# Gated linear-attention block with a gated feed-forward: output products in pairs on two row tiles, denominators in pairs, side work given to engines by a table, and a new order

## The chip, the cores and the metric

The kernel runs on one NeuronCore of a Trainium2 chip. Five engines work side by side, each through its own instructions in order: TensorE (PE in the profile, its weight loads PEld), VectorE (DVE), ScalarE (ACT), GpSimd (POOL) and SyncE (SP, which here only issues DMA). They wait for one another by semaphores. The metric is the time of one execution on the device in microseconds (us); less is better.

## The reference

Four batches (B = 4), eight heads (H = 8), 768 tokens, head size 40. Per batch and head a recurrent memory C (40 x 40) and a normaliser n are carried over the tokens, with gates that are stabilised by a running maximum m:

```
m_new  = max(f + m, i);  f_stab = exp(f + m - m_new);  i_stab = exp(i - m_new)
C = f_stab * C + i_stab * outer(v, k);   n = f_stab * n + i_stab * k
y = sigmoid(o) * (C q) / max(|n . q|, 1)
```

Then a feed-forward over x = y with the heads laid side by side (320 columns): `gate = sigmoid(causal depthwise convolution of x over 5 tokens)`, `out = (gate * (x @ w_val)) @ w_out`.

## The kernel before

The 768 tokens are cut into six blocks of 128 tokens (j0 to j5), and a block into two parts of 64 tokens (p0, p1). For each block and batch (24 pairs, u = 4j + b) the recurrence is computed part by part (g = 2u + p) in its matrix form. The scaled q and k are split into an fp16 high and low part and stacked (`prep_max`, `prep_scale`, `prep_hi`, `prep_lo`; `hi` runs on ACT or POOL, `lo` on DVE), and turned so that head channels lie on partitions, either by TensorE (`turn_pe`, copied out of PSUM by `turn_out`) or by a DMA transpose from SyncE's queue (`prep_tr`, L397); the function `TURN` says which. Then for each part: `args` (one matmul with the gate logarithms, L417), `expo` (Exp on ACT, L420), `scores` (8 matmuls, L430), `probs` (DVE, scores times decays, L435), `keyw` (POOL, keys times decays, L442), `heads` (L459 and L461: per head the output product and the update of the carried state, in two column halves of the TensorE array), and `state_out` (ACT copies the new state from PSUM back into SBUF, L468), on which the same batch's next part depends.

After both parts of a batch: `norm` (three small DVE instructions on 8 columns, L473 to L475: max(|n.q|, scale), reciprocal), `norm_o` (POOL, output gate times reciprocal, L479), `gate_o` (DVE, L482), `x_tr` (three transposes on TensorE, L489), `x_copy` (two ACT copies out of PSUM, L496 and L497).

The feed-forward of a block runs later, among the attention of later blocks: `conv` (the first of five taps on ACT, L526, the others on DVE, L528), `sigmoid`, `val` (L557 to L569), `z_mul` (DVE, L574), and per batch `outp`: two full 128-row products (L579) and the 64 channels that are left, which `outp` multiplies as a 128-row product as well for blocks j0 to j4, because `wo3` holds zeros in the other 64 rows (L581). Only in the last block, j5, which is fed in two halves of two batches, is the third product cut to 64 rows. `outp_st` (ACT, L584) copies the result to one of three buffers and `out_dma` (SyncE, L587) stores it.

The weights come as 64-bit floats and are converted on DVE, POOL and ACT (L602 to L609). Gate logarithms are built by DVE (`gates`), sent through DRAM by small DMAs on ACT's queue (`spread_g`, `spread_a`) and gathered again on SyncE's.

The whole order is written out by hand: each operation has a kind, and `PLAN` gives every instance of a kind a rank. The operations are issued in order of rank, and so each engine's queue is in that order. `BANKS` does the same for the eight PSUM banks. For most kinds the engine is fixed in the code.

## Time and profile before

| | us |
|---|---|
| median of three runs (239.35 to 240.8) | 240.64 |
| the profiled execution, its own time | 239.06 |
| span of the profiled execution, first to last instruction | 237.3 |
| busy in the span: TensorE / VectorE / ScalarE / GpSimd | 191.2 / 188.5 / 170.5 / 114.8 |
| mean granted TensorE clock, of full speed | 0.892 |

A profile is one execution. The time outside its span is 239.06 - 237.3 = 1.76 us. Matmuls are pipelined, so that TensorE counts as busy also where the next matmul could have started earlier; start-to-start distances say more than durations there. DVE instructions overlap a little as well.

### The profile page before, as it was taken

What the parts mean: (1) busy time and instruction counts of PE and PEld (TensorE: products, weight loads), DVE (VectorE), ACT (ScalarE), POOL (GpSimd) and SP (SyncE); (2) the same over time, 40 slices, a digit from 0 to 9 for tenths busy, and PEclk for the clock granted to TensorE, in tenths of its full rate; (3) what the DMA queues carried; (4) which work ended last, traced back from release to release, by engine and by line L of the source; (5) the groups of instructions that cost most, each with busy time, mean ns of one, the idle gap of its engine ahead of it and who ended that gap; (6) DMA issues with size and microseconds to landing.
All of it is one profiled execution on the core that took longest, in us unless ns stands there. A gap on an engine that the chain in (4) does not pass through costs nothing.

```text
span 237.3 us, 6304 instructions
## 1 busy us (share of the span) xinstructions
PE 191.2 (81%) x2392; PEld 138.9 (59%) x2392; DVE 188.5 (79%) x433; ACT 170.5 (72%) x353; POOL 114.8 (48%) x171
## 2 busy tenths in 40 slices
PE   0025075599951599999999999999999999999994
PEld 0024053598831576767776687677677866876541
DVE  7999989879997799789996899588966496549920
ACT  5738539978789997698998888797575827339131
POOL 8998550868877656444677184417624020220000
PEclk9999555579995555999999999999999999999999
DMA  6999955999999995999999999999794110011002
GB/s 130 155 191 163 126 79 104 181 195 123 170 181 177 179 181 75 197 175 174 197 156 187 219 179 167 211 182 157 169 172 91 42 70 3 7 51 57 3 32 79
DMA packets 146662, 31.95 MB, mean 135 GB/s; under 512 B 142472, under 2 KB 145928, under 8 KB 146632
## 3 DMA queue, kind: packets, MB, share of 16 engines
q1 hardware_dynamic: 145000, 31.25, 83.7%
q10 hardware_dynamic: 1632, 0.30, 0.9%
q8 instruction: 19, 0.31, 0.6%
q14 instruction: 11, 0.09, 0.1%
HBM read 17.87 MB, written 4.23 MB: 93 GB/s over the span
## 4 chain that ended last, share of the span: by engine, by line
PE 62%; ACT 14%; DVE 9%; issue 4%; SPq 4%; POOL 2%; DMA 2%; ACTq 1%; DVEq 0%
PE pb L459 14%; PE pb L579 12%; PE pb L560 8%; PE pb L581 6%; PE pb L557 4%; PE pb L430 4%; PE pb L562 4%; PE pb L417 3%; PE pb L569 3%; SPq L330 3%; PE pb L489 3%; ACT dm L420 2%; PE pb L461 2%; ACT stk L376 2%; DVE stk L382 2%
## 5 line engine op out<-in xcount | busy, mean ns | idle before, releaser
L459 PEld LDWEIGHTS pb<-vc,pt 104*64 104x64 f32 (+1 forms) x768 | 52.0, 148 | 10.8 <-issue 4.3
L442 POOL TENSOR_TENSOR kw<-kp,dm 128x320 f32<-128x320 f32 (+1 forms) x44 | 33.6, 770 | 49.7 <-ACT dm L420 26.3
L459 PE MATMUL pb<-vc,pt 104*64 104x41 f32 (+1 forms) x768 | 56.7, 240 | 1.0 <-ACT tq L409 0.6
L461 PE MATMUL pb<-vc,kw 128*40 128x41 f32 (+1 forms) x704 | 45.7, 222 | 5.5 <-ACT dm L420 5.5
L435 DVE SCALAR_TENSOR_TENSOR pt<-pb,cmp,dm 128x512 f32<-128x512 f32 x48 | 34.9, 744 | 12.1 <-PE pb L430 9.4
L461 PEld LDWEIGHTS pb<-vc,kw 128*40 128x40 f32 (+1 forms) x704 | 41.0, 122 | 5.7 <-POOL stk L378 5.7
L405 PE MATMUL pb<-ident,stk 128*120 128x128 f16 x96 | 12.0, 309 | 29.7 <-DVE stk L382 26.2
L378 POOL TENSOR_SCALAR stk<-nat,scl 128x640 f16<-128x640 f32 x28 | 27.3, 983 | 13.0 <-DVE scl L354 7.9
L382 DVE SCALAR_TENSOR_TENSOR stk<-nat,scl,stk 128x320 f16<-128x320 f32 x48 | 29.4, 628 | 4.7 <-POOL stk L378 2.5
L420 ACT ACTIVATE dm<-pb 128x512 f32<-128x512 f32 x48 | 27.8, 596 | 6.3 <-PE pb L417 4.1
L579 PE MATMUL pb<-wall,zt 128*128 128x320 f32 x96 | 31.0, 445 | 0.0
L528 DVE SCALAR_TENSOR_TENSOR pb<-xc,cwt,pb 128x512 f32<-128x512 f32 (+1 forms) x42 | 27.3, 668 | 2.7 <-ACT pb L526 1.9
L348 ACT ACTIVATE junk<-nat 128x320 bf16<-128x320 f32 x48 | 22.5, 469 | 9.3 <-DMA nat<-in_q_dram 5.3
L405 PEld LDWEIGHTS <-stk 128*120 128x120 f16 x96 | 10.6, 210 | 31.6 <-DVE stk L382 27.3
L468 ACT COPY vc<-pb 40x328 f32<-40x328 f32 x44 | 18.7, 425 | 13.9 <-PE pb L461 11.2
L479 POOL TENSOR_TENSOR rs<-sg,den 128x320 f32<-128x320 f32 x24 | 18.4, 769 | 19.7 <-DVE den L475 17.2
L430 PE MATMUL pb<-tq,tk 120*128 120x64 f16 x384 | 20.0, 202 | 5.6 <-ACT dm L420 4.5
L430 PEld LDWEIGHTS <-tk 120*128 120x128 f16 x384 | 17.3, 104 | 11.8 <-issue 8.2
L579 PEld LDWEIGHTS pb<-wall,zt 128*128 128x128 f32 x96 | 16.9, 190 | 6.6 <-issue 1.3
L584 ACT COPY ob<-pb 128x320 f32<-128x320 f32 x24 | 10.1, 426 | 14.4 <-PE pb L581 13.0
L560 PE MATMUL pb<-xc,wall 128*128 128x512 f32 x40 | 20.1, 625 | 0.0
L376 ACT ACTIVATE stk<-nat,scl 128x640 f16<-128x640 f32 x20 | 16.3, 827 | 5.0 <-DMA gda<-gsp 3.6
(108 smaller groups left out, 365.2 us busy)
## 6 DMA issues: line engine op xcount, KB each, us to landing
sg<-in_o_gate_dram SPq DMA_DIRECT2D x6, 640.0 KB
vc<-in_v_dram SPq DMA_DIRECT2D x12, 320.0 KB
out_dram<-ob SPq DMA_DIRECT2D x24, 160.0 KB
nat<-in_k_dram SPq DMA_DIRECT2D x10, 320.0 KB
nat<-in_q_dram SPq DMA_DIRECT2D x10, 320.0 KB
raw<-in_moe_w_val_dram SPq DMA_DIRECT2D x5, 160.0 KB
raw<-in_moe_w_out_dram SPq DMA_DIRECT2D x5, 160.0 KB
nat<-in_q_dram SPq DMA_DIRECT2D x4, 160.0 KB
```

Source lines behind the costliest of these rows:

```text
L378: nc.gpsimd.tensor_scalar(o, v, f, 1.0, op0=ALU.mult, op1=ALU.mult)
L382: nc.vector.scalar_tensor_tensor(t[:, :, lo : lo + D], part(j, x, i), scl[j % 2][:, x, i : i + 1], t[:, :, 0:D], op0=ALU.mult, op1=ALU.sub ...
L405: nc.tensor.transpose(t[0:K3, h], stack(j, x, i)[:, h, 0:K3], ident16)
L420: nc.scalar.activation(dm_[g % NDM], psd[g], AF.Exp)
L430: nc.tensor.matmul(pss[g][:, h], tk[h], tq[:, h], start=True, stop=True)
L435: nc.vector.scalar_tensor_tensor(pt_[g % NPT], pss[g], cmp_[j % 2][:, p, b : b + 1], dm_[g % NDM], op0=ALU.mult, op1=ALU.mult)
L442: nc.gpsimd.tensor_mul(kw_[g % NKW][0:n], kp[0:n, p, b * H : (b + 1) * H], dm_[g % NDM][0:n, :, L - 1 : L].to_broadcast([n, H, D]),)
L459: nc.tensor.matmul(ph[u][p * L : (p + 1) * L, h], pt_[g % NPT][0:n, h], mv, start=True, stop=True)
L461: nc.tensor.matmul(pc[g][n0 : n0 + D, h], kw_[g % NKW][0:n, h], mv, start=True, stop=True)
L528: nc.vector.scalar_tensor_tensor(of(gt, c, b0, b1) if t == 4 else o, x, w, o, op0=ALU.mult, op1=ALU.add)
L560: nc.tensor.matmul(pf, wv[:, c, ms], x[:, c, :, 4:], start=(c == 0), stop=False)
L579: nc.tensor.matmul(pf, zz[0][:, c, b], wo[:, c], start=(c == 0), stop=False)
```

## The change

- `outp` takes a pair of batches (b, b + 2) in blocks j0 to j4: first the two 128-row products of both, then the two 64-row parts one after the other, one in rows 0 to 63 of the TensorE array and one in rows 64 to 127, into two PSUM banks. Block j5 stays as it was. Ten pairs take the place of twenty single products.
- The denominator: `norm_abs` takes |n.q| on ACT, per batch; `norm_rec` takes maximum and reciprocal on DVE for two batches at once (16 columns). `norm_o` and what follows of both batches wait for the pair.
- `TURN` is true for block j0 alone: the four q tiles of j1 go by DMA transpose on SyncE's queue and no longer by TensorE and ACT.
- A table `ENG` gives instances of nineteen kinds an engine (A = ACT, V = DVE, P = POOL, S = SyncE). Before and after, in numbers of instances: `keyw` 44 POOL -> 31 POOL, 13 DVE; `rs` (`norm_o`) 24 POOL -> 15 POOL, 9 DVE; `kpe` (`load_k`) 24 POOL -> 7 POOL, 8 DVE, 9 ACT; `state` 44 ACT -> 32 ACT, 12 DVE; `xc` 24 ACT -> 12 ACT, 12 DVE; `ob` 24 ACT -> 17 ACT, 7 DVE; first taps 21 ACT -> 16 ACT, 5 DVE; `hi` 28 POOL, 20 ACT -> 22 POOL, 26 ACT; `tout` 12 ACT -> 5 ACT, 3 DVE; constants `la_c` 12 DVE -> 7 ACT, 5 DVE; `idk` 8 DVE -> 5 ACT, 1 POOL, 2 DVE; `halo` 10 copies POOL -> 2 POOL, 8 ACT; `spr` 10 ACT -> 3 ACT, 7 SyncE; `od` (stores) 24 SyncE -> 12 SyncE, 12 ACT.
- Weights load as 128-row transfers (10 instead of 14 issues); `vc` gets a row of 48 columns per head, of which 41 are used; `iota_s` is fp16; `fg` lies in memory of `sg`.
- `PLAN` and `BANKS` are new throughout. The last `heads` of j1 has rank 463 (before: 487), the last of j5 rank 1083 (before: 1073).

```diff
 def TURN(j, x, i):
-    return 1 if j == 0 or (x == 0 and j == 1) else 0
+    return 1 if j == 0 else 0
...
-    vc = ring(2, [P, 2, BH, DT], F32, "vc")
+    vc = ring(2, [P, 2, BH, DS], F32, "vc")
...
+    engines = {"A": nc.scalar, "V": nc.vector, "P": nc.gpsimd, "S": nc.sync}
+    def eng(kind, default):
+        s = ENG.get(kind)
+        return engines[s[now[1]] if s else default]
+    def copy(kind, default, out, in_):
+        e = eng(kind, default)
+        (e.copy if e is nc.scalar else e.tensor_copy)(out, in_)
...
-    def norm(u):
-        j, b = divmod(u, B)
-        d, nq = den[u % 3], ph[u][:, :, D:DT]
-        nc.vector.tensor_scalar(d, nq, -1.0, scl[j % 2][:, 0, b : b + 1], op0=ALU.mult, op1=ALU.max)
-        nc.vector.tensor_tensor(d, nq, d, op=ALU.max)
+    def norm_abs(u):
+        nc.scalar.activation(den[u // 2 % 3][:, u % 2, :, None], ph[u][:, :, D:DT], AF.Abs)
+    def norm_rec(v):
+        j, b = divmod(2 * v, B)
+        d = den[v % 3]
+        nc.vector.tensor_tensor(d, d, scl[j % 2][:, 0, b : b + 2, None].to_broadcast([P, 2, H]), op=ALU.max)
         nc.vector.reciprocal(d, d)
...
-    def outp(j, b):
-        pf = pot[j, b] = bank("outp", j * B + b, DM)
-        for c in range(2):
-            nc.tensor.matmul(pf, zz[0][:, c, b], wo[:, c], start=(c == 0), stop=False)
-        r = slice(0, P) if j < NJ - 1 else half(b)
-        nc.tensor.matmul(pf, zz[1][r, b % B2], wo3[r, b // B2], start=False, stop=True)
+    def outp(j, bs):
+        n = j * B + (2 * bs[0] if len(bs) > 1 else bs[0])
+        pf = [bank("outp", n + i, DM) for i in range(len(bs))]
+        for t, b in zip(pf, bs):
+            pot[j, b] = t
+            for c in range(2):
+                nc.tensor.matmul(t, zz[0][:, c, b], wo[:, c], start=(c == 0), stop=False)
+        for t, b in zip(pf, bs):
+            nc.tensor.matmul(t, zz[1][half(b), b % B2], wo3[half(b), b // B2], start=False, stop=True)
...
-            op("norm", norm, u)
-            op("rs", norm_o, u)
-            op("x", gate_o, u)
-            op("x_tr", x_tr, u)
-            op("xc", x_copy, u)
+            op("nabs", norm_abs, u)
+            if u % 2 == 0:
+                continue
+            op("nrec", norm_rec, u // 2)
+            for n in (u - 1, u):
+                op("rs", norm_o, n)
+                op("x", gate_o, n)
+                op("x_tr", x_tr, n)
+                op("xc", x_copy, n)
```

## Rows read from the trace of the kernel before

**Rows 1.** The page: busy time, share of the span and instructions of each engine, and the busy share of each of 40 equal slices of the span in tenths; PEclk is TensorE's granted clock in tenths of full speed.

```profile
PE 191.2 (81%) x2392; PEld 138.9 (59%) x2392; DVE 188.5 (79%) x433; ACT 170.5 (72%) x353; POOL 114.8 (48%) x171
...
PE   0025075599951599999999999999999999999994
...
DVE  7999989879997799789996899588966496549920
ACT  5738539978789997698998888797575827339131
...
PEclk9999555579995555999999999999999999999999
```

**Rows 2.** Busy time of each engine in three stretches: to the last `heads` of j1 (90.2 us), from there to the last `heads` of j5 (211.5 us), and the rest. Columns: stretch, length, busy us (instructions) by engine, granted clock, DMA share, GB/s.

```profile
0.00:90.20 90.20, 48.34 (x773) 39.92 (x774) 79.80 (x193) 70.05 (x149) 62.82 (x96) 0.74 1.07 155
90.20:211.50 121.30, 120.43 (x1538) 86.48 (x1537) 94.50 (x206) 89.86 (x180) 50.57 (x75) 0.98 0.85 140
211.50:237.30 25.80, 22.45 (x85) 12.53 (x84) 14.18 (x35) 10.55 (x25) 1.39 (x2) 1.00 0.11 39
```

**Rows 3.** The same view for four shorter stretches.

```profile
0.00:20.00 20.00, 3.76 (x32) 3.44 (x32) 18.35 (x41) 10.94 (x25) 18.05 (x39) 1.00 1.00 151
20.00:40.00 20.00, 8.60 (x68) 6.37 (x69) 18.76 (x56) 13.83 (x25) 9.56 (x13) 0.58 0.77 117
...
60.00:90.20 30.20, 19.98 (x338) 15.86 (x335) 25.92 (x61) 27.81 (x68) 21.02 (x27) 0.68 1.24 178
...
100.00:120.00 20.00, 19.91 (x286) 14.14 (x285) 18.98 (x43) 18.76 (x40) 10.35 (x15) 1.00 1.04 173
```

**Rows 4.** The page: the chain of work that ended last, as shares of the span by engine.

```profile
PE 62%; ACT 14%; DVE 9%; issue 4%; SPq 4%; POOL 2%; DMA 2%; ACTq 1%; DVEq 0%
```

**Rows 5.** The timeline of TensorE: an output product of j4 with its third part in 128 rows and what starts behind it (six transposes and the next product), and one of j5 with its third part in 64 rows and the next one behind it. Columns: start us, us, engine, line, operation, tiles, rows*columns of the array, shape, count of matmul instructions (a float32 product is two).

```profile
212.16 1.24 PE L579 MATMUL pb<-wall,zt 128*128 128x320 f32 x4
213.24 0.70 PE L581 MATMUL pb<-wall,zt 128*128 128x320 f32 x2
213.78 0.82 PE L489 MATMUL pb<-ident,x 128*128 128x128 f32 x6
214.44 1.24 PE L579 MATMUL pb<-wall,zt 128*128 128x320 f32 x4
...
225.86 1.34 PE L579 MATMUL pb<-wall,zt 128*128 128x320 f32 x4
227.13 0.80 PE L581 MATMUL pb<-wall,zt 64*128 64x320 f32 x2
227.86 1.34 PE L579 MATMUL pb<-wall,zt 128*128 128x320 f32 x4
```

**Rows 6.** The timeline of TensorE: `val` of j0's third chunk, whose twelve matmuls go alternately to two column halves of the array, and what starts behind it.

```profile
104.07 1.08 PE L569 MATMUL pb<-xc,wall 128*64 128x256 f32 x8
104.99 0.60 PE L569 MATMUL pb<-x,wall 128*64 128x256 f32 x4
105.52 0.39 PE L417 MATMUL pb<-ra,la 120*128 120x512 bf16 x1
```

**Rows 7.** The chain that ended last, in order of time (start us, us, what): four matmuls of 256 columns each on the full array.

```profile
128.54 0.86 PE pb L562 x4
```

**Rows 8.** Groups of instructions by line and shape: line, engine, operation, tiles, shapes, count, busy us, mean ns of one, idle before.

```profile
L473 DVE TENSOR_SCALAR den<-pb,scl 128x8 f32<-128x8 f32 x24 | 5.3, 221 | 6.2 <-PE pb L459 6.0
L475 DVE RECIPROCAL den<-den 128x8 f32<-128x8 f32 x24 | 4.9, 203 | 0.8
L474 DVE TENSOR_TENSOR den<-pb,den 128x8 f32<-128x8 f32 x24 | 4.0, 167 | 0.8
...
L808 DVE COPY la<-tl 120x1024 bf16<-120x1024 bf16 x6 | 4.0, 676 | 0.0
...
L574 DVE TENSOR_TENSOR zt<-pb,sg 128x256 f32<-128x256 f32 x9 | 3.7, 419 | 1.9 <-ACT sg L535 0.7 <-issue 0.6 <-PE pb L569 0.5
...
L643 DVE CAST tk<-iota_s 128x512 f16<-128x512 f32 x4 | 1.7, 415 | 0.0
...
L608 ACT ACTIVATE cv<-rawc 128x15 f32<-128x15 f32 x1 | 0.2, 218 | 0.0
```

**Rows 9.** The timeline of DVE for a stretch without waits.

```profile
102.97 0.48 DVE L482 TENSOR_TENSOR x<-pb,rs 128x320 f32<-128x320 f32 x1
103.37 0.54 DVE L382 SCALAR_TENSOR_TENSOR stk<-nat,scl,stk 128x320 f16<-128x320 f32 x1
```

**Rows 10.** `prep_lo` by its line: durations in ns, shortest, median, longest.

```profile
L382 DVE SCALAR_TENSOR_TENSOR stk<-nat,scl,stk x48: 501/546/1083, 15.6 to 172.4; 128x320 f16<-128x320 f32 x48
```

**Rows 11.** The timeline of SyncE's queue, issues of DMA: the transpose of j1's last k tile.

```profile
63.05 2.27 SPq L397 DMA_TRANSPOSE tk<-stk  x1
```

**Rows 12.** What SyncE's queue waited for: us in total, times, longest us.

```profile
SPq L587 <- ACT ob L584: 51.7, 12, 12.2
```

**Rows 13.** The timeline of the end: the table load and the two last sigmoids of j5 on ACT, the three last products on DVE, and the last copy of a result.

```profile
218.20 1.28 ACT L535 ACT_TABLE_LOAD   x1
...
225.51 1.07 ACT L535 ACTIVATE sg<-sg 128x512 f32<-128x512 f32 x2 [2.92 <-DVE sg L528]
...
226.17 1.34 DVE L574 TENSOR_TENSOR zt<-pb,sg 128x256 f32<-128x256 f32 x3 [0.69 <-ACT sg L535]
...
234.03 0.43 ACT L584 COPY ob<-pb 128x320 f32<-128x320 f32 x1 [1.58 <-PE pb L581]
```

More of the change, by code (lines that the diff above doesn't have):

```diff
@@ L128 @@
 BANKS = {
-    "turn": "132074561204",
-    "args": "230667614121475444446034170242146707542216433346",
-    "scores": "475141626526114032564774065022610545766337036114",
-    "ph": "357032503123733420725703",
-    "pc": "70224346140071222223070116241622337550061050206",
-    "x_tr": "554633013513761440415772",
-    "conv": "167546605611461216745",
-    "val": "475540176315025053621",
-    "outp": "070411550643472254237350",
-}
-def HI_ACT(j, x, i):
-    return x == 1 and j > 0
+    "turn": "10542376",
+    "args": "014313616055543100707055210314533724545722166251",
+    "scores": "256225264165631014232127505423524636006437130271",
+    "ph": "743240514732767513275167",
+    "pc": "06500710015503440020001730114344272230613020203",
+    "x_tr": "166330737311204113640550",
+    "conv": "273643126560740435106",
+    "val": "561540075534374234752",
+    "outp": "151530036434756234014304",
+}
+ENG = {
+    "c_p": "PVPPPPPPPPPPPPPPPPVPVPPP",
+    "c_v": "PPVPVPPPVVVV",
+    "idk": "AVAAPVAA",
+    "kp_c": "PA",
+    "spr": "SASAASSSSS",
+    "la_c": "AAAAAAVVVVVA",
+    "kpe": "VAVVVAAAAAAPPPPPPAVVVVPA",
+    "hi": "AAPAAAPPPAAAAAAAPPAPAAAPAAAPPAPAPPPPPPPAPPAPAAAP",
+    "tout": "VAAAAAVV",
+    "keyw": "PPPVPVPPPVVPPPVVPPPPVPPPPPVPPVPPVVVPPPPPPPVP",
+    "state": "VVVVVVAAVAAAAAAVAAVAAAAAAVAVAAAAAAAAAAAAVAAA",
+    "rs": "PPPVPPPPPVVPPVVPVPVVVPPP",
+    "xc": "VAVVVVVVAVAAVVVVAAAAAAAA",
+    "w_p": "VPVVPPPP",
+    "w_a": "AAAAAAAAAA",
+    "halo": "PPAAAAPAAAAP",
+    "conv0": "AAAVVAVAAAVAAAAAAAVAA",
+    "ob": "AAAAAAAAAAAAAVAVVVAVVAAV",
+    "od": "AAASAASSSSSAASSSASSASAAA",
+}
 def TURN(j, x, i):
-    return 1 if j == 0 or (x == 0 and j == 1) else 0
-def KP(j, p, i):
-    return 2
+    return 1 if j == 0 else 0
 @with_exitstack
@@ L259, in bank @@
         else:
-            b = turns["b"] = (turns.get("b", -1) + 1) % 8
+            own = {"ph": (0, 1), "x_tr": (2,), "args": (3,), "scores": (4,), "pc": (5,)}.get(kind, (6, 7))
+            n_ = turns[own] = turns.get(own, -1) + 1
+            b = own[n_ % len(own)]
         t = pb[b][:, 0 : n * (m or 1)]
         return t.rearrange("p (a b) -> p a b", b=m) if m else t
-    fg = cst.tile([BH, S], F32, name="fg")
+    fg = sg[0:BH, ng[0] : ng[0] + S]
     ig = cst.tile([BH, S], F32, name="ig")
@@ L275, in tile_mlstm_gated_ffn @@
     oh1 = cst.tile([P, H], BF16, name="oh1")
-    io_ = cst.tile([P, L], F32, name="iota_s")
+    io_ = cst.tile([P, L], F16, name="iota_s")
     def gates(c0, c1):
@@ L407, in turn_out @@
     def turn_out(j, x, i):
-        put = nc.scalar.copy if TURN(j, x, i) == 1 else nc.vector.tensor_copy
-        put(turned(j, x, i)[0:K3], pw[j, x, i][0:K3])
+        copy("tout", "A", turned(j, x, i)[0:K3], pw[j, x, i][0:K3])
     psd, pss, ph, pc, px = {}, {}, {}, {}, {}
@@ L613, in weights @@
         for n, w in enumerate(parts):
-            op("w_d", nc.sync.dma_start, r[n * L : (n + 1) * L], w.bitcast(I32) if wide else w)
+            r0 = n * L
+            op("w_d", nc.sync.dma_start, r[r0 : r0 + w.shape[0]], w.bitcast(I32) if wide else w)
         convert(dst, raw[i % 2], DM)
-    def two(w, c):
-        return [w[c * P + i * L : c * P + (i + 1) * L] for i in range(2)]
     def taps():
@@ L716, in feed_part @@
             op("z", z_mul, j, m, b0, b1)
[L717 to L720 removed]
+        for bs in [(b, b + B2) for b in range(B2)] if b1 - b0 == B else [(b,) for b in range(b0, b1)]:
+            op("outp", outp, j, bs)
+            for b in bs:
+                op("ob", outp_st, j, b)
+                op("od", out_dma, j, b)
     def feed(j):
```

161 lines of the change are left out of this document (80 added, 81 removed), and 69 rows, old and new, of the table PLAN.

## The prediction

> **What bounds the kernel now.** First the totals and the busy shares by slice [rows 1]. TensorE is busy 191.2 us and stands at 9 from the fifteenth slice on; before that it is half empty, and its clock lies at half speed for several slices. DVE and ACT are at 7 to 9 in the first half. Then the three stretches [rows 2], which I cut where the attention work of two blocks, and of all six, is done. To 90.2 us TensorE works 48.3 us at 0.74 of its clock; DVE works 79.8 us (88.5%), ACT 70.1. From 90.2 to 211.5 us TensorE is busy 120.4 of 121.3 us at 0.98 of its clock, DVE 94.5 (78%). The rest, 25.8 us, is TensorE with 22.5, and the last copy and store. The chain that ended last says the same: 62% of it is TensorE [rows 4]. So the first stretch is bound by the engines that prepare (DVE 93% busy over the first 40 us; ACT 27.8 of 30.2 us just before 90.2 [rows 3]), the second by TensorE alone, the third by TensorE and a latency chain. What the change is worth must be read stretch by stretch.
>
> **TensorE's part.** A single product with a 128-row third part starts at 212.16 us, its third part at 213.24, and what follows at 213.78: 1.08 + 0.54 = 1.62 us. The product of j5, whose third part has 64 rows, takes 225.86 to 227.13 to 227.86: 1.27 + 0.73 = 2.00 us [rows 5]. Both third parts stream the same columns, so 0.38 us is the price of going to 64 rows and back. The trace before has no two row halves at work together; the nearest rows are the column halves: twelve matmuls of 256 columns in 105.52 - 104.07 = 1.45 us [rows 6], where four on the whole array take 0.86 us [rows 7], or 2.58 for twelve. They run two at a time. If row halves do so, a pair costs 2 x 1.08 + 0.54 + 0.38 = 3.08 us against 3.24 for two singles: a gain of only 0.16. The bounds: without overlap 2.16 + 1.08 + 0.38 = 3.62 (a loss), without the price of the switch 2.70. I take 3.08, since rows show both of its parts. The Trainium skill, TensorEngine Tiling (Array Packing), section Key Properties, states both that a change of tiling mode drains TensorE and that different tiles run in parallel; the trace agrees with the first for rows (0.38 us) and with the second for columns. Its table under Theoretical Speedup allows a factor of two for 64 rows, by which alone the pair would be 2.70 us and ten pairs 3.8 us less than in my sum.
>
> Counted from the two order tables, the second stretch held 18 single products and now holds 10 pairs: 30.8 - 29.2 = +1.6 us, less eight entries at 0.1 (the first four matmuls take 1.34 instead of 1.24 us where the array was divided otherwise just before [rows 5]): -0.8. Four `x_tr` come in (+1.3, 0.33 each by the six transposes from 213.78 to 214.44 [rows 5]), one `val` of 1.72 + 0.86 [rows 7] goes to the first stretch (-2.6), one `args` comes (+0.2). Sum -0.3: TensorE's work in the second stretch is all but unchanged, 121.0 us at the same clock. The 2% of clock missing there are worth at most 2.4 us; the new first stretch starts `heads` earlier but still waits for DVE, so I give back half: 119.8 us. The four j1 transposes leave TensorE and ACT in the first stretch, where neither was full.
>
> **DVE's part.** Starting distance, not duration, is the price: the 320-column `x` takes 0.48 us, but the next instruction starts 0.40 after it [rows 9]. So `state`, `ob`, `keyw`, `rs` on DVE: 0.40. `xc` (256 and 128 columns): 0.52, from the 256-column product of 0.419 [rows 8] less the overlap, and half as much. `kpe` (640 columns): 0.45, between the 512-column cast's 0.415 and that times 1.25. A first tap: 0.6. `tout`, 1024 columns: 1.0 (between the 0.68 of the bfloat16 copy of that size and twice the 512-column rows). The three old denominator instructions are 0.221 + 0.167 + 0.203 = 0.59 per batch; the two new ones about 0.33 per pair [rows 8]. Abs on ACT: 0.218 by the 15-column row, 24 times 5.2 us.
>
> First stretch: 14 moved 320-column instructions (6 `keyw`, 1 `rs`, 7 `state`) 5.6, `xc` 1.6, `kpe` 1.8, `tout` 3.0, three conversions of weights 0.9, one tap 0.7, three constants 1.0; taken away: seven denominators less three new ones 3.1, copies of constants 3.4 + 1.7 + 1.0 to ACT and POOL, two `lo` 1.0. Net +4.4: 84.2 us. At the 93% that DVE kept over the first 40 us [rows 3], 90.5 us. ACT's load there is even (it loses 7 `tout` and 8 `state`, gains 9 `hi`, 6 `kpe` and 12 constants), POOL is relieved, and so the ACT jam before 90 us has no smaller load behind it. SyncE's queue gives the same end: ahead of the transpose of j1's last k tile (issued at 63.05 us [rows 11]) now stand four more transposes, w_out and more of q and k of j3, together 2.7 MB; at the stretch's 155 GB/s [rows 2] that is 17 us, 80.4 us, and some 9 us for landing, `scores`, `heads`: 89. Stores on ACT (12 of 24) shorten the 51.7 us in which SyncE stood waiting for results [rows 12]; a store on ACT costs its issue, about 0.5 us, and behind it stands the next Exp.
>
> Second stretch: 24 moved 320-column instructions 9.6, `xc` 4.7, `kpe` 1.8, first taps 2.4, seven more taps 3.5, two `lo` 0.9, denominators -8.9 + 2.6. Net +16.6: 111.1 us of 119.8, or 93%. From 100 to 120 us before, DVE was busy 18.98, ACT 18.76 and TensorE 19.91 of 20 us together [rows 3], so this can be hidden under TensorE. The new waits: Abs on ACT waits for its batch's `heads`, with the next Exp behind it; the first batch of a pair waits for the second, which costs nothing as long as the feed-forward of older blocks keeps TensorE full.
>
> Third stretch: two products (3.2 us) and two `x_tr` (0.7) less for TensorE, 21.7 us as a floor. The chain from the last `heads`: denominators 0.8, `rs`, `x`, transpose and copies of two batches 3.5, first tap 0.5, twelve taps 5.6, table load and sigmoids 1.28 + 1.07, products 1.34 [rows 13], two outputs of 2.00, last copy to the end of the span 3.2 (237.3 - 234.03): 21.3. Two limits of one size seldom fit together; I take half of the possible gain: 23.6.
>
> At nothing: whole-tile weight loads, the 48-column rows of `vc`, fp16 `iota_s`, `fg`: they save a few issues on SyncE and a fraction of one 0.415 us cast, under DVE's other work; without cover under 1 us.
>
> **Sum.** 90.5 + 119.8 + 23.6 = 233.9 us of span, + 1.76 outside = 235.7 against 239.06. The median of runs is 0.66% above this execution: 237.3 against 240.64, 1.4% less. About 1% is what a measurement can tell from no change.
>
> **Rivals.** *DVE becomes the bound.* DVE gets 195.3 us in the first two stretches. If it keeps only the 88.5% of the old first stretch, these take 220.7 us, with 24.5 after it 245.2: 248.6 us as a median, 3.3% slower. It decides from a share under 195.3 / (237.3 - 23.6) = 91.4% on. For it: 91.4% over 214 us has been reached only in parts [rows 3]. Against it: GpSimd has less to do. `prep_lo` takes 0.546 us as a rule and 1.083 at worst [rows 10], while GpSimd works; 22 instructions that move to DVE read two tiles from SBUF too, and each hit of 0.54 us would cost up to 11.9 us in all. The Trainium skill, SBUF — State Buffer, section Who interferes with whom, states that a DVE instruction with two SBUF inputs contends with a GpSimd instruction that reads SBUF and that the later one fully blocks; the trace agrees with the doubled `lo`.
>
> *The row halves don't overlap.* The change then does not do what it says: 3.62 a pair, +5.4 us: 239.3 of span, 242.6 us, 0.8% slower. Against it: the column halves do.
>
> *Everything fits.* DVE at 98% in the first stretch (85.9), no price for the switch and a warm clock in the second (121.0 - 3.8 - 2.4 = 114.8), the floor of 21.7 in the third: 222.4, 225.7 us, 6.2% faster. Against it: the first stretch held DVE at 93% at best and the transfers end near 89.
>
> **Chances.** Forecast 0.36, everything or a good part of it fits 0.28, DVE bound 0.22, no overlap 0.09, else 0.05 (counted as slower). The forecast, 1.4% under, falls half into faster (0.18) and half into the same (0.18). Faster 0.18 + 0.28 = 0.46; same 0.18 + 0.02 of DVE bound + 0.05 of no overlap = 0.25; slower the rest, 0.29. The range is 228 to 247: it leaves out the far half of the good case (about 0.08) and of the DVE case (about 0.1). The forecast's own range is 234 to 241.
>
> **What would show it.** TensorE's distance from the third part of a pair to the next instruction: 0.54 + 0.38 (right), over 1.2 (no overlap). DVE busy near 207 us; its share to the last `heads` of j1 and of j5, near 90 and 210 us; TensorE's busy share between them near 99%, with waits for `probs` and `rs` if DVE has become the bound. It would be wrong above all if the new order starves TensorE in the second stretch, or if it fills the first.

## The result: slower by 0.8%

| | before | after |
|---|---|---|
| median of 20 runs, us | 239.33 (237.85 to 240.8) | 241.38 (240.1 to 242.82) |
| ratio, 95% interval | 1 | 1.0081 [1.0057, 1.0105] |
| profiled execution, us (its span) | 239.06 (237.3) | 240.3 (238.4) |
| TensorE busy / DVE busy, us | 191.2 / 188.5 | 187.8 / 211.0 |

The forecast was 237.3 us, 1.4% less than before; the kernel became 0.8% slower. That lies in the range and within the 1% called no change, but the interval is clear of 1: a small loss, and of the other sign than the forecast. Ratios and their intervals, here and below, leave out executions that took over 1.5% longer than the kernel's fastest; medians count all.

The page of the changed kernel, to be held against [rows 1] and [rows 4]:

```profile
PE 187.8 (79%) x2360; PEld 131.8 (55%) x2360; DVE 211.0 (89%) x453; ACT 171.2 (72%) x358; POOL 75.7 (32%) x118
...
PE   0011489477578874988999999998999999999994
...
DVE  7999999999999997989999999999999499677840
ACT  7794789999389999697686987698945645555220
...
PEclk9999999979955895999999999999999999999999
...
PE 44%; DVE 35%; issue 7%; ACT 6%; POOL 4%; DMA 2%; SPq 1%; POOLq 0%; DVEq 0%; ACTq 0%
```

DVE took over part of GpSimd's work (GpSimd 114.8 us before, 75.7 now) and stands at 9 in all but two of the slices from the second to the thirty-first. The chain has turned from 62% TensorE and 9% DVE to 44% and 35%. The same three stretches as in [rows 2], cut at the last `heads` of j1 and j5, and the second one in three pieces (busy us of PE, PEld, DVE, ACT, POOL, then clock, DMA share, GB/s):

```profile
0.00:86.50 86.50, 47.99 (x742) 37.87 (x743) 81.77 (x190) 71.91 (x151) 33.56 (x63) 0.90 1.07 158
86.50:216.30 129.80, 121.23 (x1555) 84.25 (x1554) 117.70 (x238) 92.81 (x194) 40.71 (x54) 0.97 0.87 142
216.30:238.40 22.10, 18.58 (x67) 9.68 (x66) 11.56 (x28) 6.50 (x14) 1.40 (x2) 1.00 0.10 37
...
86.50:100.00 13.50, 8.60 (x52) 5.06 (x53) 12.00 (x30) 11.27 (x21) 7.35 (x10) 0.75 1.26 181
100.00:180.00 80.00, 76.33 (x1134) 54.42 (x1131) 77.05 (x155) 63.04 (x137) 30.02 (x39) 1.00 1.09 172
180.00:216.30 36.30, 36.30 (x373) 24.77 (x371) 28.64 (x55) 18.51 (x38) 3.33 (x5) 1.00 0.22 62
```

Against the sum of the prediction, the first stretch came out at 86.5 us (90.5 forecast), the second at 129.8 (119.8), the third at 22.1 (23.6): -4.0 + 10.0 - 1.5 = +4.5, which is 238.4 - 233.9. The second stretch holds the error. TensorE works 121.23 us there and stands idle for 8.57: 4.90 from 86.5 to 100 us, 3.67 from 100 to 180, nothing after that.

Beside before it is best counted from a common point in time. The same view to 100 us, to 180 and to the end, first of before:

```profile
0.00:100.00 100.00, 57.70 (x885) 46.39 (x886) 87.74 (x213) 75.83 (x163) 67.65 (x103) 0.74 1.05 153
100.00:180.00 80.00, 79.57 (x1041) 56.57 (x1041) 67.65 (x144) 68.41 (x136) 39.62 (x56) 1.00 1.14 179
180.00:400.00 220.00, 53.95 (x475) 35.97 (x470) 33.09 (x77) 26.23 (x56) 7.51 (x12) 1.00 0.03 11
```

and of after:

```profile
0.00:100.00 100.00, 56.59 (x792) 42.92 (x794) 93.77 (x218) 83.18 (x171) 40.92 (x72) 0.88 1.09 161
...
180.00:400.00 220.00, 54.88 (x438) 34.45 (x436) 40.21 (x82) 25.01 (x52) 4.73 (x7) 1.00 0.05 14
```

Behind 100 us TensorE has 131.21 us of work left (133.52 before), a gain of 2.31. But it idles 238.4 - 100 - 131.21 = 7.19 us (3.78 before), a loss of 3.41, and 3.24 of that lies between 100 and 180 us. The balance is the +1.1 us of span. So the question is what TensorE waits for where it all but never waited before. The view of TensorE's waits from 100 to 180 us names 3.4 us, none longer than 0.6 (what waited, for what; us in total, times, longest):

```profile
PE pb L482 <- DVE pt L458: 1.4, 4, 0.6
PE pb L482 <- ACT vc L268: 0.6, 1, 0.6
PE pb L453 <- DVE pt L458: 0.4, 1, 0.4
PE pb L484 <- DVE zt L604: 0.4, 1, 0.4
PE pb L453 <- DVE vc L268: 0.3, 1, 0.3
PE pb L590 <- DVE pt L458: 0.3, 1, 0.3
```

Here 2.8 of the 3.4 us name DVE, 2.1 of these the `probs` (`pt`). Somewhat over half are waits for an operand (`heads`, L482, for `probs` or a state), the rest for a bank that an engine has not yet read. Three from the timeline of TensorE (in brackets the idle time before it, and what ended it), behind the two long ones that lie right after j1's heads:

```profile
90.94 0.58 PE L440 MATMUL pb<-ra,la 120*128 120x512 bf16 x1 [2.48 <-DVE x L268]
93.41 1.01 PE L453 MATMUL pb<-tq,tk 120*128 120x64 f16 x16 [1.89 <-DMA tq<-stk]
94.23 2.98 PE L590 MATMUL pb<-xc,wall 128*128 128x512 f32 x4
...
102.50 0.25 PE L482 MATMUL pb<-vc,pt 104*64 104x41 f32 x1 [0.63 <-ACT vc L268]
...
121.76 1.99 PE L590 MATMUL pb<-xc,wall 128*128 128x512 f32 x4 [0.33 <-DVE pt L458]
...
159.56 0.25 PE L482 MATMUL pb<-vc,pt 128*64 128x41 f32 x1 [0.57 <-DVE pt L458]
```

From 100 to 180 us DVE is busy 77.05 of 80 us, where it was 67.65, and from 86.5 to 180 us the view of DVE's waits names 2.3 us (some 12 before). ACT is busy 63.04 us there, less than the 68.41 of before. Read by itself this says that DVE has become the bound. The experiments were made to test that.

### The profile page after: what moved, and what is told of

Its sections match the earlier page's. It is cut to its first block, busy times and chain, and to the rows that moved or that the text cites. A ratio compares the mean times of both kernels' runs of the same rounds, so it can differ in the third digit from the quotient of the medians.

```text
span 238.4 us, 6170 instructions
## 1 busy us (share of the span) xinstructions
PE 187.8 (79%) x2360; PEld 131.8 (55%) x2360; DVE 211.0 (89%) x453; ACT 171.2 (72%) x358; POOL 75.7 (32%) x118
## 3 DMA queue, kind: packets, MB, share of 16 engines
q10 hardware_dynamic: 1896, 1.99, 3.1%
## 4 chain that ended last, share of the span: by engine, by line
PE 44%; DVE 35%; issue 7%; ACT 6%; POOL 4%; DMA 2%; SPq 1%; POOLq 0%; DVEq 0%; ACTq 0%
PE pb L612 11%; PE pb L482 8%; DVE pt L458 5%; DVE stk L406 4%; PE pb L587 4%; PE pb L614 4%; PE pb L590 4%; DVE pb L558 4%; PE pb L453 3%; PE pb L440 3%; DMA sg<-in_o_gate_dram 2%; ACT junk L372 2%; PE pb L599 2%; PE pb L592 2%; DVE kw L465 2%
## 5 line engine op out<-in xcount | busy, mean ns | idle before, releaser
L482 PE MATMUL pb<-vc,pt 104*64 104x41 f32 (+1 forms) x768 | 56.9, 240 | 6.4 <-DVE vc L268 2.4
L482 PEld LDWEIGHTS pb<-vc,pt 104*64 104x64 f32 (+1 forms) x768 | 51.9, 147 | 14.8 <-ACT vc L268 3.8
L465 POOL TENSOR_TENSOR kw<-kp,dm 128x320 f32<-128x320 f32 (+1 forms) x31 | 23.2, 754 | 38.7 <-ACT dm L443 17.9
L402 POOL TENSOR_SCALAR stk<-nat,scl 128x640 f16<-128x640 f32 x22 | 18.2, 831 | 47.7 <-DMA tq<-stk 18.5
L612 PE MATMUL pb<-wall,zt 128*128 128x320 f32 x96 | 29.1, 443 | 0.1
L429 PE MATMUL pb<-ident,stk 128*120 128x128 f16 x64 | 8.4, 318 | 26.1 <-DVE stk L406 26.0
L504 POOL TENSOR_TENSOR rs<-sg,den 128x320 f32<-128x320 f32 x15 | 11.9, 807 | 44.3 <-DVE den L500 27.2
L400 ACT ACTIVATE stk<-nat,scl 128x640 f16<-128x640 f32 x26 | 21.1, 825 | 3.5 <-DVE scl L378 3.0
L590 PE MATMUL pb<-xc,wall 128*128 128x512 f32 x40 | 22.1, 682 | 0.3 <-DVE pt L458 0.3
L429 PEld LDWEIGHTS <-stk 128*120 128x120 f16 x64 | 7.2, 218 | 27.0 <-DVE stk L406 27.0
L440 PE MATMUL pb<-ra,la 120*128 120x512 bf16 x48 | 19.0, 413 | 2.7 <-DVE x L268 2.5
L268 ACT COPY vc<-pb 40x328 f32<-40x328 f32 x32 | 13.8, 432 | 7.0 <-PE pb L484 6.2
```

What stands on the lines that cost most here:

```text
L440: nc.tensor.matmul(psd[g], la[:, p, j, b], ra[:, :, j], start=True, stop=True)
L465: eng("keyw", "P").tensor_mul(kw_[g % NKW][0:n], kp[0:n, p, b * H : (b + 1) * H], dm_[g % NDM][0:n, :, L - 1 : L].to_broadcast([n, H, D]),)
L482: nc.tensor.matmul(ph[u][p * L : (p + 1) * L, h], pt_[g % NPT][0:n, h], mv, start=True, stop=True)
L590: nc.tensor.matmul(pf, wv[:, c, ms], x[:, c, :, 4:], start=(c == 0), stop=False)
L612: nc.tensor.matmul(t, zz[0][:, c, b], wo[:, c], start=(c == 0), stop=False)
```

## The experiments

All are variants of the kernel after, unless they are called variants of before. The ratio is to the kernel before, run on the same chip; spans and busy times (us) are those of one profiled execution (of e7 only times are given).

| | ratio, 95% interval | median | span | PE busy | DVE busy | PE busy 100 to 180 |
|---|---|---|---|---|---|---|
| before | 1 | 239.33 | 237.3 | 191.2 | 188.5 | 79.57 |
| after | 1.0081 [1.0057, 1.0105] | 241.38 | 238.4 | 187.8 | 211.0 | 76.33 |
| e1_late_home | 1.0109 [1.0068, 1.0151] | 242.38 | 240.6 | 187.6 | 192.8 | 75.31 |
| e2_singles | 1.0175 [1.0136, 1.0215] | 243.93 | 242.1 | 191.4 | 212.3 | 76.82 |
| e3_same_half | 1.0251 [1.0208, 1.0294] | 245.57 | 243.1 | 193.9 | 211.2 | 78.25 |
| e4_old_den | 1.0263 [1.022, 1.0305] | 246.33 | 244.3 | 191.5 | 217.6 | 74.39 |
| e5_pairs_alone (of before) | 1.0437 [1.0396, 1.0478] | 249.87 | 247.8 | 189.0 | 189.5 | 73.26 |
| e6_den_alone (of before) | 1.0449 [1.0412, 1.0485] | 250.46 | 249.8 | 192.0 | 185.6 | 74.85 |
| e7_pairs_den (of before) | 1.0834 [1.0781, 1.0887] | 260.57 | | | | |
| e8_sides_alone (of before) | 1.0636 [1.06, 1.0672] | 254.84 | 252.7 | 194.7 | 210.4 | 74.77 |
| e9_keyw_pool | 1.0038 [1.0008, 1.0068] | 240.91 | 239.0 | 190.1 | 209.9 | 78.23 |
| e10_engines | 1.0205 [1.0166, 1.0245] | 244.36 | 242.8 | 191.9 | 208.2 | 77.29 |
| e11_order | 1.0326 [1.0278, 1.0373] | 247.38 | 245.7 | 192.0 | 212.4 | 73.36 |
| e12_both | 1.0492 [1.0449, 1.0534] | 251.73 | 247.7 | 193.6 | 206.3 | 73.27 |
| e13_less_taps | 1.0043 [1.0011, 1.0076] | 240.86 | 239.2 | 189.8 | 191.9 | 78.12 |
| e14_before_taps (of before) | 0.9988 [0.9964, 1.0011] | 239.38 | 237.6 | 188.8 | 168.7 | 79.58 |
| e15_less_max | 1.0043 [1.0018, 1.0067] | 240.7 | 238.5 | 191.2 | 210.7 | 77.44 |
| e16_eight | 1.0034 [1.0, 1.0067] | 241.09 | 239.5 | 190.7 | 208.1 | 76.74 |
| e17_less_both | 1.001 [0.9992, 1.0027] | 239.7 | 237.7 | 191.3 | 191.4 | 78.44 |
| e18_after_again | 1.0073 [1.0049, 1.0097] | 241.29 | 238.7 | 190.9 | 211.3 | 77.32 |

**Undoing one part of after.** e1 sends 39 of the moved instructions, from j1's last products on, back to the engine that had them.

```
-    "kpe": "VAVVVAAAAAAPPPPPPAVVVVPA",
+    "kpe": "VAVVVAAAAAAPPPPPPAPPPPPA",
...
-    "xc": "VAVVVVVVAVAAVVVVAAAAAAAA",
+    "xc": "VAVVAAAAAAAAAAAAAAAAAAAA",
```

> The kernel after with its order and banks, but from the last products of j1 on, the 39 side instructions that the engine table gives to DVE go back to where the kernel before had them (keyw, rs and the copies of k to GpSimd; xc, state and first taps to ACT). Theory 1, DVE's own load paces the stretch from 86 to 180 us: DVE busy falls from 211 to about 190 us, TensorE's waits between 100 and 180 us (3.7 us in the kernel after) fall below 1.5, and the time falls by 2.5 to 5 us, to 236.5 to 239. Theory 2, the new order itself brings operands late, whoever makes them: the waits of TensorE keep their size within 1 us and the time stays at 241.4 within 1 us. Theory 3, GpSimd and ACT are as full as DVE: slower than 242.

DVE lost 18.2 us of work and 14.7 us of that in 100 to 180 us, and nothing was won: the interval covers after's ratio, and TensorE stands idle for 4.69 us from 100 to 180, where theory 1 had said under 1.5. The same windows row of e1, and its longest wait of TensorE behind 86.5 us (us in total, times, longest):

```profile
100.00:180.00 80.00, 75.31 (x1134) 53.85 (x1131) 62.40 (x116) 67.03 (x156) 39.90 (x54) 1.00 1.10 171
```

```profile
PE pb L440 <- ACT x L268: 5.0, 3, 3.2
```

The copies that TensorE waits for now stand in ACT's queue, and cost 5.0 us there. The longest of the three, 3.2 us, is the one that took 2.5 us with the copy on DVE: in e1 the copy starts at 90.91 us, behind a table load and the sigmoid of an output gate that hold ACT from 87.68. So the loss is not DVE's load alone, at least not in a way that goes when the work stands in other queues.

e2 computes each product by itself again, with a third weight tile of 128 rows half of which is zero; e3 keeps the pairs, but of batches that share a row half.

```
-            nc.tensor.matmul(t, zz[1][half(b), b % B2], wo3[half(b), b // B2], start=False, stop=True)
+            nc.tensor.matmul(t, zz[1][r, b % B2], wo3[r, b // B2], start=False, stop=True)
```

```
-        for bs in [(b, b + B2) for b in range(B2)] if b1 - b0 == B else [(b,) for b in range(b0, b1)]:
+        for bs in [(2 * b, 2 * b + 1) for b in range(B2)] if b1 - b0 == B else [(b,) for b in range(b0, b1)]:
```

> The kernel after with the ten pairs of output products undone: each batch by itself, third part on all 128 rows with zeros in the other half of the weights (two more fills on GpSimd). By the trace of after a pair takes 2.99 to 3.09 us from its start to the next instruction, two singles took 3.24 to 3.44 before. If pairs pay what they show, TensorE is busy 2.5 to 4 us longer; where TensorE sets the pace (half of the ten lie behind 180 us) this comes out in the time, where DVE does it is hidden: slower by 1 to 3 us, 242.4 to 244.4. If the pairs are what made the kernel after slow (waits for two products' buffers and copies at once): faster, below 241.

> The kernel after, but with the pairs formed of neighbours (batches 0 and 1, 2 and 3), whose third parts stand on the same 64 rows of the array. If the two halves of a pair really run side by side in the kernel after, the two third parts now follow each other: a pair takes 3.5 to 3.65 us instead of 2.99 to 3.09, TensorE gets 4.5 to 6 us more work, and the time rises by 2 to 5 us. If they did not overlap in the kernel after, nothing changes: the pair stays at 3.0 to 3.1 us and the time at 241.4 within 1.

The timeline of TensorE shows one pair of each with what starts behind it: after (two row halves),

```profile
184.43 2.32 PE L612 MATMUL pb<-wall,zt 128*128 128x320 f32 x8
186.68 0.81 PE L614 MATMUL pb<-wall,zt 64*128 64x320 f32 x4
187.42 0.41 PE L453 MATMUL pb<-tq,tk 120*128 120x64 f16 x8
```

e3 (one half twice),

```profile
187.00 2.32 PE L612 MATMUL pb<-wall,zt 128*128 128x320 f32 x8
189.24 1.34 PE L614 MATMUL pb<-wall,zt 64*128 64x320 f32 x4
190.52 0.41 PE L453 MATMUL pb<-tq,tk 120*128 120x64 f16 x8
```

and e2 (two whole products):

```profile
186.69 1.24 PE L613 MATMUL pb<-wall,zt 128*128 128x320 f32 x4
187.77 0.70 PE L614 MATMUL pb<-wall,zt 128*128 128x320 f32 x2
188.31 1.24 PE L613 MATMUL pb<-wall,zt 128*128 128x320 f32 x4
189.38 0.70 PE L614 MATMUL pb<-wall,zt 128*128 128x320 f32 x2
```

From the third parts to the next instruction it takes 0.74 us in after and 1.28 in e3: the two row halves run side by side, and of the second third part nothing is left but 0.74 - 0.54 = 0.20 us. Counted over the whole pair, as the prediction counted its 0.38, the price of the switch is 2.99 - 2.70 = 0.29 us, and 0.40 in the dearest pair (3.10). A pair is 187.42 - 184.43 = 2.99 us (others reach 3.10), against 3.52 in e3 and 2 x 1.62 = 3.24 for two singles at their cheapest. By their starts in the timelines the ten pairs took 30.5 us in all in after and 35.8 in e3, the twenty singles 33.5 in e2 and 33.8 in before (1.61 to 1.81 each). e3 adds 5.3 us to TensorE and is slower than after by 1.0251 - 1.0081 = 1.7%, 4.1 us; e2 adds 3.0 us and is slower by 0.94%, 2.2 us. In both some three quarters of what is added to TensorE reach the end, and both came out as forecast. TensorE is then still what the time hangs on, and the pairs are a gain.

e4 takes the denominators back to three DVE instructions per batch.

```
-        nc.scalar.activation(den[u // 2 % 3][:, u % 2, :, None], ph[u][:, :, D:DT], AF.Abs)
+        nc.vector.tensor_scalar(d, nq, -1.0, scl[j % 2][:, 0, b : b + 1], op0=ALU.mult, op1=ALU.max)
+        nc.vector.tensor_tensor(d, nq, d, op=ALU.max)
+        nc.vector.reciprocal(d, d)
```

> The kernel after with the denominators of the kernel before: three DVE instructions per batch where ACT's Abs stood, and nothing where the pair's maximum and reciprocal stood. That is 24 x 0.59 us more on DVE and 12 x 0.41 less, 9.2 us net, 24 x 0.2 less on ACT. Theory 1 (DVE paces the kernel until 180 us): about 7 of the 9.2 us lie before that and come out, slower by 3 to 7 us, 244.5 to 248.5. Theory 2 (the order, not the load): within 1.5 us of 241.4. If ACT's Abs in front of the next Exp is what costs: faster.

DVE gets 6.6 us more work, and the kernel is 4.4 us (1.82%) slower than after, as theory 1 had forecast. In after's order, then, two thirds of what the new denominators free on DVE reach the end, where e1 gained nothing by moving nearly three times as much off it. The old instructions stand here in an order that was made for the new ones, so a misfit may be in the 4.4 us.

**One part alone, in the order of before.** e5 takes the pairs over, e6 the denominators, e7 both, e8 the engines of `keyw`, `rs`, `state`, `xc` and `kpe`; the order is that of before but for the entries that have to go together. In e6 two tiles that are in use at once come to share a bank twice (the arguments of j2's batch 3 with a product of j0, and a product of j0 with a state of j2), so that these values are lost; the instructions are the same, but waits for the shared banks may be in its time.

```
-        r = slice(0, P) if j < NJ - 1 else half(b)
-        nc.tensor.matmul(pf, zz[1][r, b % B2], wo3[r, b // B2], start=False, stop=True)
+        for t, b in zip(pf, bs):
+            nc.tensor.matmul(t, zz[1][half(b), b % B2], wo3[half(b), b // B2], start=False, stop=True)
```

```
-    def norm(u):
+    def norm_abs(u):
+        nc.scalar.activation(den[u // 2 % 3][:, u % 2, :, None], ph[u][:, :, D:DT], AF.Abs)
...
+    def norm_rec(v):
```

```
-        nc.gpsimd.tensor_mul(
+        eng("keyw", "P").tensor_mul(
...
-        nc.scalar.copy(dst[n0 : n0 + D, b * H : (b + 1) * H], pc[g][n0 : n0 + D])
+        copy("state", "A", dst[n0 : n0 + D, b * H : (b + 1) * H], pc[g][n0 : n0 + D])
```

> The kernel before with its own order, engines and denominators, and only the output products of the first five blocks in pairs (the pair stands where one of its two products stood; one bank moved). Ten pairs at 3.04 us take the place of twenty products at 1.66 us: TensorE has 2.8 us less to do, all of it behind 100 us, where it was never idle before. If the parts of the change pay and its order and engine table take the gain away: 1.5 to 3 us faster, 236.5 to 238.5. If a pair's need of two banks and two copies at once costs what it saves: within 1 us of the kernel before.

> The kernel before with only the denominators changed: ACT's Abs per batch where the three DVE instructions stood, maximum and reciprocal once per pair behind the second batch, rs and what follows for the first batch moved behind it. DVE gets 9 us less (24 x 0.59 less 12 x 0.41), ACT 4.8 us more. Behind 93 us TensorE is full and DVE has room, so only the first stretch can gain (eight batches, 3 us of DVE): 0 to 2 us faster if DVE's load sets it. If the first batch's wait for the second, or Abs in front of the next Exp, costs: slower by 0.5 to 2 us.

> The kernel before with both of these edits and nothing else of the change. If the parts pay by themselves and the order and the engine table spoil it: 2 to 4 us faster than before, 235.5 to 237.5. If not: within 1 us of the kernel before.

> The kernel before in its own order, with keyw, rs, state, xc and the copies of k on the engines of the new table (54 of them on DVE, some 29 us by the durations of the trace of after: 13 x 0.49, 9 x 0.56, 12 x 0.46, 12 x 0.64, 8 x 0.55). DVE would be busy 217 of 238 us. If DVE's load matters: slower by 3 to 8 us. If only the order matters, and a fuller DVE costs nothing as long as the work stands in the right places: within 1.5 us of before.

Every part alone loses, and more than the whole: against the 240.06 us of before on their chip +9.8, +10.4, +20.0 and +14.8 us, where all of it with the new order costs 2.0. All four forecasts missed. In e5 TensorE is even busy 2.2 us less than before (at a mean granted clock of 0.972 against 0.892, so this is not work alone), and yet the span grows by 10.5. The timeline of ACT shows one place (e5):

```profile
111.50 0.75 ACT L584 COPY ob<-pb 128x320 f32<-128x320 f32 x2 [1.46 <-PE pb L581]
```

ACT reaches the copy of a result at the place where the single product had been done; the pair ends later, and ACT stands for 1.46 us with maxima and copies of states queued behind it. From 100 to 180 us it stands 7.4 us in this way, in five places (1.2 us in before), and TensorE is busy 73.26 of 80 us; its waits there name `probs`, a state and results not yet copied. That the one brings the other is read from the queues and not tested. As I read them, these four runs don't price the parts: they price an order that was written for other durations.

**Other engines and orders for after.** e9 moves eight `keyw` from DVE to GpSimd, e16 eight entries of four kinds off DVE. e10 takes a new engine table (kinds `kpe`, `hi`, `keyw`, `state`, `rs`, `xc`, `conv0`, `ob`, `od`), e11 a new order, e12 both; they came out of a replay of after's instructions with the durations of its trace, in which they ended earlier than after.

```
-    "keyw": "PPPVPVPPPVVPPPVVPPPPVPPPPPVPPVPPVVVPPPPPPPVP",
+    "keyw": "PPPVPVPPPVVPPPVPPPPPPPPPPPPPPPPPPPPPPPPPPPPP",
```

```
-    "rs": "PPPVPPPPPVVPPVVPVPVVVPPP",
+    "rs": "PPPVPPVPVPVPPPPVPPVVPVPV",
```

```
-    "ld_v": "115 142 249 277 424 402 532 601 690 746 865 829",
+    "ld_v": "115 142 249 277 424 402 615 560 721 812 948 809",
```

> The kernel after, with 8 instructions moved and nothing else: keyw from the last batch of j1 on stands on GpSimd throughout, which is 28% busy there, and no more on DVE; each is read by heads, so it lies on the chain of the attention blocks, and on DVE it stands in a full queue. Theory 1b: it is not DVE's total load that costs (the run with 39 instructions sent home showed that), but chain work that stands behind other work in a full queue; then these 8 alone take back 1.5 to 3.5 us (a replay of the queues in order, with the durations and delays of the trace of after, which gives its own end within 1 us, says 3.3): 238 to 240. If GpSimd's longer keyw (0.75 against 0.49 us) is what a chain feels: slower by 0 to 2 us.

> The kernel after in its own order, but with the side work of j2 to j5 dealt to the engines anew: 68 entries of the engine table changed by a search over that replay (keyw to GpSimd and most of rs too, four of the xc copies, three first taps and four states between DVE and ACT exchanged, eight of hi, stores between ACT and SyncE). The replay ends 5.3 us earlier than that of after. If the engine table is what the change lost by: 3 to 6 us faster than after, 235.5 to 238.5. If it is the order: within 1.5 us of after.

> The kernel after with its engine table, banks and work, but with the order of the operations from 82 us on searched anew over the same replay (no operation passes one that it depends on). The replay ends 3.5 us earlier. If the order is what the change lost by: 2 to 4 us faster than after, 237.5 to 239.5. If the engine table is: the order can't mend it, within 1.5 us of after.

> Both at once: order and engines from 82 us on searched together; same work, same pairs and denominators, same banks. The replay ends 8.8 us earlier than that of after. If the parts of the change pay once order and engines fit them: 5 to 9 us faster than after, 232.5 to 236.5, and so faster than both kernels. If the replay misses what costs on the chip: no better than after.

> The kernel after with eight entries of its engine table changed, all of them off DVE between 108 and 185 us: keyw of j2 b2 p0, j3 b1 p0, j4 b0 p0 and j4 b1 p0 and one copy of k to GpSimd; xc of j3 b0 and b3 and one first tap to ACT (some 4.2 us off DVE). Each stands where a probs, a state or an x that TensorE waits for comes right behind it. The replay ends 3.5 us earlier. Theory 1: 1.5 to 3.5 us faster, 238 to 240, equal to before or faster. If what each queue gains the other loses: within 1 us of 241.4.

The two small moves stand 0.4% to 0.5% under after's first ratio, with intervals that overlap its own, and above their forecasts of 238 to 240 us. The three large ones are 3 to 10 us slower than after, where the replay had them 3.5 to 8.8 us faster. One thing that the replay had not got right is the transposes by DMA: GpSimd's queue in e10 stands 5.89 us for one of them in a `prep_hi`, a `keyw` waits behind it, and TensorE's state product waits for that (timelines of GpSimd and TensorE):

```profile
163.63 1.13 POOL L412 TENSOR_SCALAR stk<-nat,scl 128x640 f16<-128x640 f32 x1 [5.89 <-DMA tq<-stk]
164.73 1.71 POOL L475 TENSOR_TENSOR kw<-kp,dm 104x320 f32<-104x320 f32 x2
...
165.51 0.29 PE L494 MATMUL pb<-vc,kw 104*40 104x41 f32 x1 [1.28 <-POOL kw L475]
```

That this is the larger part of the miss is not shown: in e11 the two longest waits of TensorE from 86.5 to 180 us are for a copy on DVE (2.2 us) and an Exp on ACT (2.1).

**Taking work away instead of moving it.** A moved instruction lands in another queue. So e13 leaves out three of the four taps per channel group of j1 to j4 (36 DVE instructions), e14 does so in before, e15 leaves out ACT's maxima of j2 to j5, e17 does both, and e18 is after, unchanged, beside e17.

```
-                op("conv" if t else "conv0", conv, n, j, c, t, b0, b1)
+                skip = 1 <= j <= 4 and 0 < t < 4
+                op("conv" if t else "conv0", (lambda *a: None) if skip else conv, n, j, c, t, b0, b1)
```

```
-                    op("max", prep_max, j, x, i)
+                    op("max", prep_max if j < 2 else (lambda *a: None), j, x, i)
```

> The kernel after with taps 1 to 3 of the convolution left out for blocks j1 to j4 (36 DVE instructions, some 22 us; the result of these blocks lacks three of five taps); nothing else is moved. Theory 1, DVE's full queue holds TensorE back until 180 us: TensorE's waits between 100 and 180 us (3.7 us named by the profile, some 6 us against its full pace) go to less than a third and the time falls by 3 to 5 us, to 236.5 to 238.5. Theory 2, the order, the two-bank pairs or ACT hold it: within 1 us of 241.4.

> The kernel before with the same 36 taps left out. Behind 93 us TensorE never waited there for more than 0.5 us and DVE was 78% busy. If only a queue that is nearly full holds TensorE back, nothing is gained: within 1 us of before. If it gains as much as the kernel after does (3 us or more), the taps' own place on the way to z, not DVE's load, is what the cut relieves, and the run on the kernel after tells nothing about load.

> The kernel after without the absolute maxima of q and k for j2 to j5 (32 pairs of instructions on ACT, some 19 us; the scales of these blocks are those of older ones); the control to the run without taps. Theory 1: ACT is not what TensorE waits for behind 95 us, within 1 us of 241.4 (before 95 us a few of them may help: up to 1.5 faster). Theory 2, ACT's queue is the one that is late: 3 us or more faster.

> The kernel after without taps 1 to 3 of j1 to j4 and without the absolute maxima of j2 to j5 (22 us off DVE and 19 us off ACT together; results of these blocks differ accordingly). Theory load: either queue steps in for the other, and with both relieved TensorE's waits behind 100 us, 5.9 us over the usual length of its operations in the kernel after, fall below 1.5 and the time by 4 us or more, to 237 or less. Theory spacing: the waits come from steps of one chain that stand too close in TensorE's order (heads, the copy of its state, heads; scores, probs, heads; a bank written again two operations later); they stay above 2.5 us and the time above 239.

> The kernel after, unchanged, beside the run above: 1.008 of before as in its own job, if the chips of the jobs treat it alike. If it comes out at 1.003 to 1.005 here, the runs without taps, without maxima and with eight moved instructions gained nothing; if at 1.008 or more, they gained about 0.4%.

The windows row for 100 to 180 us, in this order: e13, e15, e17, e18.

```profile
100.00:180.00 80.00, 78.12 (x1150) 55.88 (x1149) 64.74 (x132) 63.27 (x138) 30.11 (x39) 1.00 1.14 175
```

```profile
100.00:180.00 80.00, 77.44 (x1143) 55.17 (x1143) 76.94 (x155) 54.64 (x105) 30.20 (x39) 1.00 1.12 173
```

```profile
100.00:180.00 80.00, 78.44 (x1146) 55.79 (x1146) 65.12 (x134) 55.22 (x106) 30.62 (x39) 1.00 1.10 173
```

```profile
100.00:180.00 80.00, 77.32 (x1143) 55.08 (x1140) 77.19 (x155) 63.26 (x137) 30.01 (x39) 1.00 1.11 172
```

After by itself idles 2.68 us here (e18; 3.67 in its first profile), without the taps 1.88, without the maxima 2.56, without both 1.56, before 0.43. These are single executions, and two of the same kernel differ by 1.0 us; what carries the argument is the times. They are 1.0073 in e18 and 1.001 in e17, on one chip and with intervals that don't touch, so some 37 us less busy time on DVE and ACT (211.3 to 191.4, and 171.7 to 154.6) bring back 0.63%, or 1.5 us. What TensorE waited for from 100 to 180 us in e17, to be held against the same view of after:

```profile
PE pb L440 <- DVE zt L604: 0.7, 2, 0.5
PE pb L590 <- DVE pt L458: 0.3, 1, 0.3
PE pb L482 <- DVE pt L458: 0.2, 1, 0.2
PE pb L453 <- DVE vc L268: 0.2, 1, 0.2
```

The waits for `probs` have gone from 2.1 us in after (1.7 in e18) to 0.5. By the marks set beforehand neither theory of e17 is met: load asked for 237 us or less, spacing for more than 239 us with waits that stay. It became 239.7 us, but the waits have shrunk. And an instruction that is left out shortens the chain in which it stands as well as its queue; no run here tells the two apart. Singly, either cut brings 0.3% to 0.4%, about the width of the intervals, where theory 1 of e13 had forecast 3 to 5 us. In before the same taps are worth nothing (0.9988 [0.9964, 1.0011]): there TensorE already works 79.57 of the 80 us. The maxima were not taken out of before.

## Why the prediction was wrong

**What held.** TensorE's part, in the main: a pair at 2.99 to 3.10 us (3.08 said). Off were the singles, for which I took the 1.62 us of a cheap one: the twenty took 33.8 us, so the ten pairs saved 3.3 us and not 1.6. The 121.0 us that I gave for TensorE's work in the second stretch was taken from the length of the stretch, idle time included; from its 120.4 us of work it would be 120.1, and it measured 121.23, with 1.0 us too much in one slow `val` (below). The rival without overlap is refuted by e3, although its number, 242.6 us, lies nearest to the result: a number can be right by another mechanism. The third stretch took 22.1 us, between my floor and my value. DVE was busy 211.0 us (207 said). The prices were start-to-start distances; by these `ob`, `state` and the shorter `keyw` (104 rows) did take 0.40 us, but `rs` took 0.62 (median of the four with no wait behind them), and the 128-row `keyw` 0.55 on average: two tiles from SBUF were priced too low. The groups of DVE after, by duration (mean ns of one behind the busy time):

```profile
L465 DVE TENSOR_TENSOR kw<-kp,dm 128x320 f32<-128x320 f32 x7 | 4.4, 633 | 0.1
...
L504 DVE TENSOR_TENSOR rs<-sg,den 128x320 f32<-128x320 f32 x9 | 5.3, 591 | 0.2
...
L268 DVE COPY xc<-pb 128x256 f32<-128x256 f32 x12 | 4.9, 411 | 0.0
...
L268 DVE COPY x<-pb 64x128 f32<-64x128 f32 x12 | 3.3, 276 | 0.1
```

An Abs on ACT took 172 ns (218 said). The good case needed DVE at 98% in the first stretch; it was 94.5% (81.77 of 86.5 us), near the 93% of the forecast.

**The step that failed** is the sentence on DVE's part in the second stretch: "so this can be hidden under TensorE", with its companion, that a wait in a pair "costs nothing as long as the feed-forward of older blocks keeps TensorE full". I compared sums: 111.1 us of DVE work fit into 119.8. They did, 117.7 into 129.8. But TensorE's queue is in order, and it takes each `probs`, state and `z` at one place. With DVE at 96% and ACT at 79% from 100 to 180 us, little idle time is left in which a delayed instruction could catch up, and TensorE stands for it. These waits, which I had set to nothing, measured 3.67 and 2.68 us in two executions, where before had 0.43. Beside them, 1.2 us that I had taken off for a warmer clock did not come: from 86.5 to 100 us TensorE was granted 0.75 of its clock, and the four matmuls of a `val` from 94.23 us took 2.98 us, where those from 121.76 us took 1.99.

**The rest of the 10 us** is the hole right behind the first stretch, 4.90 us (4.10 in e18). The last `heads` of j1 came 4.0 us earlier than forecast, but what comes next was not ready: the copy of a transposed x, which the table moved to DVE and which stands there behind two taps and a conversion of weights, and the transpose of q of j2, issued together with another in 5.41 us of SyncE's queue. One thing I had not looked at: the new order puts one `sig_o`, the sigmoid of an output gate, behind the last `heads` of j1 (rank 480, before 420). With a table load on either side it holds ACT from 87.86 to 91.90 us in after, and from 74.94 to 78.79 in before, where TensorE then waited 5.54 us for the Exp behind it. So a part of the earlier end may be idle time that only changed sides of the cut. What is left for TensorE behind 100 us says the same: 2.31 us less than before, and the pairs alone save 3.3 there, so that by 100 us after has done no more than before (busy 56.59 us, 58.47 in e18, against 57.70, but at 0.88, 0.85 and 0.74 of the clock). So the earlier end of the first stretch was no gain. No run here closed that hole (the variants of after are busy 8.0 to 9.9 of these 13.5 us; e1, with the copy on ACT, 8.07), and none moved `sig_o` back: its cause is read from the trace and not shown.

**DVE as the bound**, the first rival, was priced at 248.6 us for a share of DVE of 88.5%, and was to decide below 91.4%. The share to 216.3 us is (81.77 + 117.70) / 216.3 = 92.2%, but the 91.4% came from 195.3 us of work. With the 199.5 us measured and the 22.1 us behind them it would be 199.5 / (237.3 - 22.1) = 92.7%, so the rule settles nothing. e1 and e13 do: with 18 to 19 us less work on DVE the kernel gains 0.4% at most, about half of its loss, so DVE alone isn't it. Shown is this: without some 37 us of the work of DVE and ACT the kernel gets back 1.5 of the 1.8 us by which after was slower than before on that chip (e17 against e18). That it is the fullness of the queues, and not the shorter chains, is argued; ACT was no fuller than before from 100 to 180 us, DVE was. Shown too is that pairs and denominators, undone, cost 2.2 and 4.4 us in this order. Not settled is what the new order would be worth by itself, or how much of the missing gain is the hole and how much the spacing of the queues; my attempts at a better order (e10 to e12) all lost, and no variant of after beat before.
